# DMA transposes for q and x, smaller stores on GpSimd's queue, and row tiles of 128 in a fused attention and convolution kernel

**The chip, the cores and the metric.** One core of a Trainium2 chip. The metric is the device time of one execution in microseconds (us). With one core a run is called fast or slow by its own kernel only: slow is more than 1.5% above the fastest run of the same kernel. A ratio is the mean time of one kernel's fast runs over that of the other's of the same rounds, so it is not quite the ratio of the medians that are quoted. A run's first figure is the median of all its runs, slow ones too.

## The reference

Eight batches of linear attention (8 heads, 576 rows, 64 columns) feed a gated long convolution over the 576 rows. Cut to what matters:

```python
def phi(x, c, s):                       # c, s: cos and sin of pi/2 * row / 576
    r = np.maximum(x, 0.0)
    return np.concatenate([r * c, r * s], axis=-1)
kv  = einsum('bhsf,bhsd->bhfd', phi(k), v);  z = phi(k).sum(axis=2)
num = einsum('bhsf,bhfd->bhsd', phi(q), kv)
x   = (num / (phi(q) @ z + 1e-6)).transpose(0, 2, 1, 3).reshape(B, S, 512)
x1, x2, x3 = split(x @ w_proj, 3)
y   = x1 * irfft(rfft(x2) * rfft(filter)) * x3
out = y @ w_out                         # (8, 576, 512), float32
```

## The kernel before

Each batch goes through one pipeline: loads on GpSimd's queue (they cast to 16 bits), phi on VectorE, the transposes of q on TensorE, num, a "fold" of the attention result into frequency order (which also gives the x of the gate), x2, dft, the gate matmuls, the inverse, y, out, and stores. The parts that the change and the argument touch:

```python
def load_qk(b, nm, hs=slice(0, NH)):
    ...                                              # one load of 96 partitions
    nc.gpsimd.dma_start(out=raw_t[(b, nm)][:, hs],
        in_=src[b, hs].rearrange("h (p j) d -> p h (j d)", j=NJ))

def emit_qt(b, hp):                                  # q: transposed on TensorE, 12 of them
    for hh in range(2):
        for j in range(NJ):
            nc.tensor.transpose(u[:, hh, ds(j * NP, NP)], qp[:, j, 2 * hp + hh]..., perm)
    ...                                              # then two copies out of PSUM

def emit_out(b, grps=OG):
    ov = out[b].rearrange("(p j) n -> j p n", j=6)
    ...
        os_ = late["p"].tile([128, ng, DM], FP32, tag=f"os{ng}", bufs=2 * ng, ...)
    ...                                              # at most 96 rows, one leading dimension
            src = os_[x - OT[t] : e - OT[t], t - grp[0]]
            dst = ov[jb, p_a:p_b]
            q_ = nc.scalar if b >= B - 2 and t % 2 == 1 else nc.sync
            q_.dma_start(out=dst, in_=src)
```

Of the kernel before, what the change touches and what calls it, by code (L numbers as in the profile page):

```python
# [17 lines left out]
def kernel(  # L18
# [15 lines left out]

    nc = tc.nc
# [6 lines left out]
    NT = 5  # L42
# [25 lines left out]
    tcol = consts.tile([128, NJ], FP32, tag="tcol", name="tcol")  # L68
    epsc = consts.tile([128, NT], FP32, tag="epsc", name="epsc")
    perm = consts.tile([NP, NP], FP16, tag="perm", name="perm")  # L70
# [5 lines left out]
    fm = consts.tile([128, 24, 10], FP16, tag="fm", name="fm")  # L76
    tre = consts.tile([NP, 3, NP], FP16, tag="tre", name="tre")
    tim = consts.tile([NP, 3, NP], FP16, tag="tim", name="tim")

# [9 lines left out]
    qpt_buf = [consts.tile([128, NH, NT, 2, 64], FP16, tag=f"qpt{i}", name=f"qpt{i}") for i in range(1)]  # L89
# [24 lines left out]
    raw_t = {}  # L114

    def load_qk(b, nm, hs=slice(0, NH)):
        src = {"q": q, "k": k, "v": v}[nm]
        if hs.start == 0:
            rw = work.tile([NP, NH, NJ * D], FP16, tag="raw", bufs=4, name=f"{nm}raw{b}")
            raw_t[(b, nm)] = rw  # L120
        nc.gpsimd.dma_start(
            out=raw_t[(b, nm)][:, hs], in_=src[b, hs].rearrange("h (p j) d -> p h (j d)", j=NJ)
        )

    def emit_va(b, xs=range(4)):
        for x in xs:
            hs = slice(2 * x, 2 * x + 2)
            nc.scalar.copy(  # L128
                out=va_buf[b % 2][:, hs, :, 0:D],
                in_=raw_t[(b, "v")][:, hs].rearrange("p h (j d) -> p h j d", j=NJ),  # L130
            )
# [28 lines left out]
    def emit_iotas(part):  # L160
# [13 lines left out]
        iota("sr_i", [NP, QS], lambda t: [(t, [[2, 3], [12, NP // 2]], 1, 0)])  # L174

    def emit_cols():
# [6 lines left out]
        nc.vector.memset(warm, 0.0)  # L183
        sj = cc["s6_i"]
# [3 lines left out]
        nc.vector.tensor_tensor(out=tcol, in0=tcol, in1=scol, op=AL.mult)  # L188

        u16 = small("u16p")  # L190
        rnd(u16, p, 1.0 / 16.0, -15.0 / 32.0)
        dest = small("dest")
        tsc(dest, p, 6.0, AL.mult)
        nc.vector.scalar_tensor_tensor(
            out=dest, in0=u16, scalar=-95.0, in1=dest, op0=AL.mult, op1=AL.add
        )
        tsc(perm, cc["nrow_i"], dest[0:NP], AL.is_equal)

    def emit_pads():
        for va in va_buf:  # L200
            nc.vector.memset(va[:, :, :, D : D + 2], 1.0 / A1)
        for t in qpt_buf:
            nc.vector.memset(t[:, :, :, 0, 60:64], 0.0)
            nc.vector.memset(t[:, :, :, 1, 0:4], 0.0)

    def emit_fm():

        p = cc["p"]
        loc = small("loc")
        side = small("side")  # L210
        nc.vector.tensor_copy(out=loc[0:64], in_=p[0:64])
        tsc(loc[64:128], p[64:128], -1.0, AL.mult, 127.0, AL.add)
        nc.vector.memset(side[0:64], 1.0)
        nc.vector.memset(side[64:128], -1.0)
        lo = small("lo")
        rnd(lo, loc, 1.0 / 6.0, -5.0 / 12.0)
        li = small("li")
        nc.vector.scalar_tensor_tensor(
            out=li, in0=lo, scalar=-6.0, in1=loc, op0=AL.mult, op1=AL.add
# [3 lines left out]
        orb = small("orb", NT)  # L223
        for t in range(NT):
            tsc(orb[:, t : t + 1], lo, 10.0 * t, AL.add)
        oj = small("oj", NT)
        rnd(oj, orb, 1.0 / 16.0, -15.0 / 32.0)
        pos = small("pos", NT)

        tsc(pos, orb, 6.0, AL.mult)  # L230
        nc.vector.scalar_tensor_tensor(
            out=pos, in0=oj, scalar=-95.0, in1=pos, op0=AL.mult, op1=AL.add
        )
        nc.vector.scalar_tensor_tensor(
            out=pos, in0=li.to_broadcast([128, NT]), scalar=96.0, in1=pos, op0=AL.mult, op1=AL.add
        )
# [6 lines left out]
        orow_i = cc["orow_i"][:, 0:10]  # L243
        match = small("match", 10)
# [5 lines left out]
        for sl, (kk, c0) in enumerate([(0, 0.25), (3, 0.25), (1, 0.25), (1, 0.0), (2, 0.25), (2, 0.0)]):  # L250
# [4 lines left out]
        nc.scalar.activation(out=coef[:, 0:6], in_=ph, func=AF.Sin, scale=TWO_PI)  # L255
        tsc(coef[:, 3:6:2], coef[:, 3:6:2], 1.0 / R3, AL.mult)

        tsc(coef[:, 0:6], coef[:, 0:6], 2.0, AL.mult)
        tsc(coef[:, 0:6], coef[:, 0:6], RC, AL.add, -RC, AL.add)
        tsc(coef[:, 0:6], coef[:, 0:6], 0.5, AL.mult)  # L260
        tsc(coef[:, 6:12], coef[:, 0:6], side, AL.mult)
# [12 lines left out]
            in0=coef.unsqueeze(2).to_broadcast([128, 24, 10]),  # L274
            in1=match.unsqueeze(1).to_broadcast([128, 24, 10]),
# [23 lines left out]
    def emit_rows():  # L299
# [5 lines left out]
        par = cc["par"] = small("par")  # L305
        rnd(par, p, 0.5, -0.25)
        nc.vector.scalar_tensor_tensor(
            out=par, in0=par, scalar=-2.0, in1=p, op0=AL.mult, op1=AL.add
        )
# [10 lines left out]
    def emit_fwd_tables():  # L320
# [4 lines left out]
        u = small("u16")  # L325
        rnd(u, p, 1.0 / 16.0, -15.0 / 32.0)
        j = small("jr")
        nc.vector.scalar_tensor_tensor(
            out=j, in0=half, scalar=-3.0, in1=u, op0=AL.mult, op1=AL.add
        )  # L330
        w = small("w2s")

        tsc(w, p, 12.0, AL.mult, 1.0, AL.add)
        nc.vector.scalar_tensor_tensor(out=w, in0=u, scalar=-192.0, in1=w, op0=AL.mult, op1=AL.add)
        nc.vector.scalar_tensor_tensor(out=w, in0=j, scalar=2.0, in1=w, op0=AL.mult, op1=AL.add)
# [24 lines left out]
        for tb in (tre, tim):  # L360
            tsc(tb[:, 1:3], tb[:, 1:3], amp[0:NP], AL.mult)
            nc.vector.tensor_tensor(out=tb[:, 0], in0=tb[:, 0], in1=mask, op=AL.mult)

# [59 lines left out]
    def emit_h():  # L423
        hc, hs_, hb, alt = cc["hc"], cc["hs"], cc["hb"], cc["alt"]
        fa = filt16.rearrange("p x (j n) -> p x j n", j=3)
        for x, op in ((0, AL.add), (1, AL.subtract)):
            with behind("phi", 1, "k"):
                nc.vector.tensor_tensor(
                    out=feo[:, x].rearrange("p j n -> p (j n)"),
                    in0=filt16[:, 0], in1=filt16[:, 1], op=op,  # L430
                )
        for bl in range(3):
# [15 lines left out]
            tsc(h3[:, bl, 1], u[0:NP, 1], sc, AL.mult)  # L448
            nc.vector.tensor_copy(out=h3[:, bl, 2], in_=h3[:, bl, 1])
        u = unit("h_nyq")  # L450
        for j in range(3):
            nc.tensor.matmul(
                u[0:1, 0], alt[:, j % 2 : j % 2 + 1], feo[:, 0, j], start=(j == 0), stop=(j == 2)
            )
        nc.scalar.activation(out=h3[0:1, 0, 2], in_=u[0:1, 0], func=AF.Copy, scale=1.0 / S)
# [4 lines left out]
    def emit_phi(b, nm, h0=0, nh=NH):  # L460
        rw = raw_t[(b, nm)]
        dst = kp_t if nm == "k" else qp_t
        if h0 == 0:
            dst[b] = work.tile([NP, NJ, NH, 2, D], FP16, tag=f"{nm}p", bufs=2 if nm == "q" else 1, name=f"{nm}p{b}")
        t = dst[b]
        if nm == "q":

            tsc(
                t[:, :, h0 : h0 + nh, 0],
                rw[:, h0 : h0 + nh].rearrange("p h (j d) -> p j h d", j=NJ), 0.0, AL.max,  # L470
            )
        for j in range(NJ):
            for cs, col in ((0, ccol), (1, scol)) if nm == "k" else ((1, tcol),):
                mark["phi", b, nm] = tsc(
                    t[:, j, h0 : h0 + nh, cs], rw[:, h0 : h0 + nh, ds(j * D, D)],
                    col[0:NP, j : j + 1], AL.mult, 0.0, AL.max,
                )
# [20 lines left out]

    def emit_qt(b, hp):
        qp, qpt = qp_t[b], qpt_buf[0]  # L500
        u = psum.tile([128, 2, 1024], FP16, tag="u", bufs=4, name=f"qt{b}_{hp}")
        for hh in range(2):
            for j in range(NJ):
                nc.tensor.transpose(  # L504
                    u[:, hh, ds(j * NP, NP)],
                    qp[:, j, 2 * hp + hh].rearrange("p a b -> p (a b)"),
                    perm,
                )
        hsl = slice(2 * hp, 2 * hp + 2)
        ev = nc.scalar.copy if b == 0 and hp < 2 else nc.vector.tensor_copy  # L510
        mark["qpt", b, hp] = ev(  # L511
            out=qpt[:, hsl, :, 0, 0:60],
            in_=u[:, :, 0:300].rearrange("p h (t c) -> p h t c", c=60),
        )
        nc.scalar.copy(  # L515
            out=qpt[:, hsl, ::-1, 1, 4:64],
            in_=u[:, :, 276:576].rearrange("p h (t c) -> p h t c", c=60),
        )

    def emit_num(b, hp, wm=0):  # L520
        qpt, kvs = qpt_buf[0], kvs_t[b]
        if hp == 0:
            att_t[b] = work.tile([128, NT, DM], FP16, tag="att", bufs=2, name=f"att{b}")
# [3 lines left out]
        for hh in range(2):  # L527
            h = 2 * hp + hh
            for t in range(NT):
                nc.tensor.matmul(  # L530
                    u[:, hh, ds(t * 65, 65)], qpt[:, h, t].rearrange("p a b -> p (a b)"),
                    kvs[:, h // 4, ds((h % 4) * 65, 65)], start=True, stop=True,
                )
        nv = u[:, :, 0 : NT * 65].rearrange("p h (t e) -> p h t e", e=65)
        rcp = work.tile([128, 2, NT], FP32, tag="rcp", bufs=2, name=f"rcp{b}_{hp}")
        nc.vector.tensor_tensor(
            out=rcp, in0=nv[:, :, :, 64], in1=epsc.unsqueeze(1).to_broadcast([128, 2, NT]), op=AL.add
# [5 lines left out]
            in1=rcp.unsqueeze(3).to_broadcast([128, 2, NT, D]),  # L543
# [3 lines left out]
    def emit_fx(b, cs=range(NC), ccs=None, wm=0):  # L547
        att = att_t[b]
        if 0 in cs:
            fx_t[b] = work.tile([128, NC, 24, 48], FP16, tag="fx", bufs=2, name=f"fx{b}")  # L550
        fx = fx_t[b]
        for c in cs:
            u = unit(f"fx{b}_{c}")
            warm_up(u, wm)
# [325 lines left out]
```

## Time and profile before

| | before |
|---|---|
| time, median of 4 runs beside the changed kernel | 272.1 us (269.4 to 272.2) |
| start, first batch, four more batches, tail | 68.8, 30.3, 4 x 28.5, 58.1 us |
| TensorE, VectorE, ScalarE busy | 90%, 84%, 73% |

The batches are cut where the 48 small kv matmuls begin. The page's row of the DMA engines' busy share in 40 slices of the span, in tenths:

```profile
DMA  5999998919019296636860868114000600060235
```

### The profile page before, as it was taken

How to read it: one execution, taken by the hardware profiler on the slowest of the kernel's cores; microseconds unless marked ns; L12 is line 12 of the kernel's file. 1: busy time of each engine (PE TensorE's matmuls, PEld its weight loads, DVE VectorE, ACT ScalarE, POOL GpSimd, SP SyncE). 2: the span in 40 equal slices, each digit the busy share in tenths (PEclk: the TensorE clock that was granted, in tenths of full speed). 3: DMA queues.
4: the chain of work that ended last, by engine and by line, in shares of the span. 5: the costliest groups of instructions: out<-in, count | busy, mean ns of one | idle time of the engine just before them, and what ended most of it. 6: DMA issues, size and time to landing. Idle time of an engine off the chain costs nothing.

```text
span 271.2 us, 6320 instructions
## 1 busy us (share of the span) xinstructions
PE 243.0 (90%) x2457; PEld 175.2 (65%) x2457; DVE 226.9 (84%) x805; ACT 196.8 (73%) x274; POOL 27.3 (10%) x47
## 2 busy tenths in 40 slices
PE   0287998878989999999999999999999999999991
PEld 0164767547858776786678676867687768756830
DVE  7689997998899898979897989978997479646951
ACT  2279679798497778877897789786977667857630
POOL 8551111020020101110111011000000000000000
PEclk9999999995799999999999999999999999999998
DMA  5999998919019296636860868114000600060235
GB/s 79 168 206 205 206 205 122 166 14 169 3 14 161 33 230 90 89 40 152 150 101 3 174 128 124 16 51 125 0 2 9 169 2 0 2 174 13 69 117 155
DMA packets 26991, 26.70 MB, mean 98 GB/s; under 512 B 1680, under 2 KB 22160, under 8 KB 26960
## 3 DMA queue, kind: packets, MB, share of 16 engines
q0 software_dynamic: 21200, 16.84, 42.7%
q1 hardware_dynamic: 5120, 8.39, 10.7%
q10 hardware_dynamic: 640, 1.05, 1.3%
q8 instruction: 19, 0.31, 0.5%
q14 instruction: 12, 0.10, 0.1%
HBM read 33.69 MB, written 9.44 MB: 159 GB/s over the span
## 4 chain that ended last, share of the span: by engine, by line
PE 50%; ACT 22%; DVE 21%; DMA 4%; issue 1%; POOL 0%; SPq 0%; POOLq 0%; ACTq 0%
PE x L630 20%; PE x L593 9%; ACT x2f L598 7%; ACT va L128 7%; PE kv L491 5%; PE out L695 4%; PE fx L556 4%; DVE eo L672 4%; ACT fx L560 3%; DMA vraw<-in_v_dram 2%; DVE kp L99 2%; PE qt L504 2%; PE dft L607 2%; PE inv L657 2%; DVE qpt L511 2%; PE inv L656 2%
## 5 line engine op out<-in xcount | busy, mean ns | idle before, releaser
L630 PE MATMUL x<-fx,wp 128*128 128x288 f16 x512 | 67.5, 286 | 1.1 <-ACT fx L560 1.0
L630 PEld LDWEIGHTS <-wp 128*128 128x128 f16 x512 | 50.0, 98 | 13.3 <-issue 0.3
L593 PE MATMUL x<-wp,fx 128*96 128x512 f16 x192 | 45.2, 382 | 0.5 <-ACT x2f L598 0.5
L560 ACT CAST fx<-fx 128x960 f16<-128x960 f32 x32 | 30.6, 961 | 13.7 <-PE fx L556 13.7
L695 PE MATMUL out<-wo,y 128*128 128x512 f16 x160 | 37.6, 379 | 0.7 <-DVE y L677 0.7
L598 ACT ACTIVATE x2f<-x 96x1024 f16<-96x1024 f32 x24 | 24.5, 1020 | 14.6 <-PE x L593 14.6
L593 PEld LDWEIGHTS <-fx 128*96 128x96 f16 x192 | 22.4, 124 | 15.1 <-issue 0.8
L672 DVE TENSOR_TENSOR eo<-eq 128x144 f16<-128x144 f16 x128 | 23.7, 228 | 10.1 <-ACT eq L660 9.9
L128 ACT COPY va<-vraw 96x768 f16<-96x768 f16 x32 | 25.3, 827 | 9.3 <-DMA vraw<-in_v_dram 9.3
L638 DVE TENSOR_TENSOR g<-x,x1s 128x288 f16<-128x288 f32 x64 | 27.0, 448 | 1.3 <-PE x L630 1.1
L491 PE MATMUL kv<-va,kp 96*128 96x65 f16 x384 | 16.4, 202 | 11.7 <-ACT va L128 8.8
L540 DVE TENSOR_TENSOR att<-num,rcp 128x640 f16<-128x640 f32 x32 | 26.1, 820 | 0.3
L515 ACT COPY qpt<-qt 128x600 f16<-128x600 f16 x32 | 20.4, 671 | 7.5 <-DVE qpt L511 7.5
L695 PEld LDWEIGHTS <-y 128*128 128x128 f16 x160 | 14.9, 97 | 16.0 <-DVE y L677 1.2
L609 ACT CAST xf<-dft 96x1024 f16<-96x1024 f32 x24 | 23.5, 1010 | 2.2 <-PE dft L607 1.2
L491 PEld LDWEIGHTS <-kp 96*128 96x128 f16 x384 | 15.3, 104 | 13.3 <-DVE kp L99 8.1
L504 PEld LDWEIGHTS <-qp 96*128 96x128 f16 x384 | 20.2, 102 | 5.1 <-issue 1.1
L636 ACT CAST x1s<-x 128x576 f16<-128x576 f32 x32 | 20.5, 639 | 4.2 <-PE x L630 3.1
L612 DVE TENSOR_TENSOR m<-xf,h 96x1024 f16<-96x1024 f16 x24 | 16.3, 678 | 7.8 <-ACT xf L609 7.7
L504 PE MATMUL qt<-perm,qp 96*128 96x96 f16 x384 | 21.7, 213 | 0.5 <-ACT fx L560 0.3
L700 ACT ACTIVATE os<-out 128x1024 f32<-128x1024 f32 (+1 forms) x21 | 18.3, 883 | 5.2 <-PE out L695 5.1
L556 PE MATMUL fx<-fm,att 128*128 128x240 f16 x128 | 18.8, 270 | 2.2 <-DVE att L540 1.1
(185 smaller groups left out, 419.4 us busy)
## 6 DMA issues: line engine op xcount, KB each, us to landing
out_dram<-os SPq DMA_DIRECT2D x22, 192.0 KB, 2.5
qraw<-in_q_dram POOLq DMA_DIRECT2D x7, 576.0 KB, 6.6
kraw<-in_k_dram POOLq DMA_DIRECT2D x7, 576.0 KB, 6.3
vraw<-in_v_dram POOLq DMA_DIRECT2D x7, 576.0 KB, 6.5
out_dram<-os SPq DMA_DIRECT2D x20, 128.0 KB, 2.4
wp<-in_moe_w_proj_dram POOLq DMA_DIRECT2D x3, 512.0 KB, 12.3
out_dram<-os SPq DMA_DIRECT2D x22, 64.0 KB, 2.1
kraw<-in_k_dram POOLq DMA_DIRECT2D x2, 288.0 KB, 6.4
```

What stands on the lines that cost most here:

```text
L128: nc.scalar.copy(out=va_buf[b % 2][:, hs, :, 0:D], in_=raw_t[(b, "v")][:, hs].rearrange("p h (j d) -> p h j d", j=NJ),)
L491: nc.tensor.matmul(u[:, h // 4, ds((h % 4) * 65, 65)], kp[:, j, h].rearrange("p a b -> p (a b)"), va[:, h, j, 0:65], start=(j == 0), stop= ...
L504: nc.tensor.transpose(u[:, hh, ds(j * NP, NP)], qp[:, j, 2 * hp + hh].rearrange("p a b -> p (a b)"), perm,)
L540: mark["att", b, hp] = nc.vector.tensor_tensor(out=att[:, :, ds(hp * 128, 128)].rearrange("p t (h d) -> p h t d", h=2), in0=nv[:, :, :, 0: ...
L556: nc.tensor.matmul(u[:, t // 2, 0:480].rearrange("p (g o) -> p g o", o=20)[:, :, ds((t % 2) * 10, 10)], att[:, t, ds(c * 128, 128)], fm, s ...
L560: nc.scalar.copy(out=fx[:, c, :, 0:40].rearrange("p g (u o) -> p u g o", u=2), in_=u[:, :, 0:480].rearrange("p u (g o) -> p u g o", o=20),)
L593: nc.tensor.matmul(u[0:NP, comp], fx[:, c, ds(comp * 6 + 2 * bl, 2)].rearrange("p a b -> p (a b)"), wp16[:, c, ds(DM, DM)], start=(c == 0) ...
L598: mark["x2f", b, bl] = nc.scalar.mul(out=x2f[:, bl], in_=u[0:NP], mul=X2SC)
L630: nc.tensor.matmul(u[:, hf, 0:HS], wp16[:, i, ds(w * DM + c * 128, 128)], fx[:, i, ds(12 + 6 * hf, 6)].rearrange("p a b -> p (a b)"), star ...
L638: mark["g", b, c] = nc.vector.tensor_tensor(out=(g[:, c, 0:HS] if hf == 0 else g[:, c, HS:S][:, ::-1]).rearrange("p (j i o) -> p j i o", j ...
L672: nc.vector.tensor_tensor(out=eoh[:, a, :, ds(48 * x, 48)], in0=eqj[:, a, 0], in1=eqj[:, a, 1], op=op)
L695: nc.tensor.matmul(u[:, x], y[:, c, ds(OT[t], 128)], wo16[:, c], start=(c == 0), stop=(c == NC - 1),)
```

## The change

The intent is to take work off TensorE: q's 48 transposes and the fold's part for x go to DMA transposes, x2 uses full 128-row tiles, and narrow matmuls are put in pairs into different column groups. For this q is loaded with the even and the odd of its groups of six rows in separate partitions and transposed in 48-row pieces. The output rows of a row tile then belong to an even and an odd half, so the stores become smaller and more, and they move to GpSimd's queue. The core of a long diff (set-up tables, tile shapes and the order of emission are cut):

```diff
+    DMA_XT = 2
+    DMA_QT = 2
 def load_qk
+        if nm == "q" and b >= DMA_QT:
+            for e in range(2):
+                nc.gpsimd.dma_start(out=rw[ds(64 * e, 48), hs], in_=view[e::2])
 def emit_qt(b, hp)
+        if b >= DMA_QT:
+            e, half = hp % 2, hp // 2
+            nc.sync.dma_start_transpose(
+                out=qpt.rearrange("p h (j e m n) -> p (h j) e m n", ...)[:, :, e, half],
+                in_=qp[ds(64 * ((e + half) % 2), 48), half].rearrange("p h j a b -> p (h j a b)"))
+            return
+    def emit_xt(b):
+        nc.sync.dma_start_transpose(out=xt_t[b]..., in_=att_t[b]...)
 def emit_out
-        ov = out[b].rearrange("(p j) n -> j p n", j=6)
+        ov = out[b].rearrange("(k x y) n -> x y k n", x=2, y=6)
-                [128, ng, DM], FP32, tag=f"os{ng}", bufs=2 * ng, ...
+                ... FP32, tag="osl" if last else f"os{ng}", bufs=5 if last else ng, ...
-                    q_ = nc.scalar if b >= B - 2 and t % 2 == 1 else nc.sync
+                    q_ = nc.gpsimd if b < B - 2 else nc.sync
+                    if e - pos == 96:
+                        q_.dma_start(out=ov[:, m // 2], in_=sv[pos - OT[t] : e - OT[t]])
+                    elif t < 4 or last:
+                        q_.dma_start(out=ov[m % 2, m // 2, k0 : k0 + e - pos], in_=...)
+                    else:                            # 64 rows in two column halves
+                        for hf in range(2): q_.dma_start(...)
```

## The prediction

> **What bounds the kernel now.** I read the page first (busy shares), then the chain that ended last in order of time, then one table of windows cut at its repeating landmarks, then the groups by form inside one such window.
>
> ```profile
> PE 243.0 (90%) x2457; PEld 175.2 (65%) x2457; DVE 226.9 (84%) x805; ACT 196.8 (73%) x274; POOL 27.3 (10%) x47
> ```
>
> TensorE (PE) is busiest, but 90% of the span hides what happens in the middle. The chain shows a repeat: the 48 small kv matmuls come back every 28.5 us (127.58, 156.08, 184.58, 213.08). One repeat is one of the 8 batches.
>
> ```profile
> 94.41 0.51 PE qt L504 x12
> 94.92 1.73 PE out L695 x8
> ...
> 127.58 1.69 PE kv L491 x48
> 129.27 1.76 PE x L593 x8
> ...
> 137.45 1.96 PE x L630 x16
> 139.41 0.41 PE fx L556 x4
> ...
> 156.08 1.68 PE kv L491 x48
> ...
> 216.51 0.61 PE num L530 x20
> ...
> 259.38 1.03 ACT os L700
> 260.75 0.43 issue
> 261.61 2.06 DMA out_dram<-os
> 263.67 0.60 ACT os L702
> 264.30 0.70 DVE os L97
> 265.02 1.89 DMA out_dram<-os
> 266.91 0.69 DVE os L97
> ```
>
> A chain piece with a count gives the pitch, which is what a stream of overlapping matmuls really costs: 16 gate matmuls of 288 columns in 1.96 us are 0.1225 us each, though the groups give 286 ns as the mean of one. The windows, cut at the kv times, then give each engine's load in a batch (columns: us, PE, PEld, DVE, ACT, POOL busy with counts, clock, DMA share, GB/s):
>
> ```profile
> core 0: us, PE busy (x) PEld busy (x) DVE busy (x) ACT busy (x) POOL busy (x), PEclk, DMA share, GB/s
> 0.00:68.79 68.79, 51.02 (x531) 36.57 (x532) 61.00 (x265) 48.12 (x75) 18.51 (x36) 0.95 1.00 152
> 127.58:156.08 28.50, 27.89 (x302) 20.67 (x302) 25.68 (x85) 23.03 (x32) 2.32 (x3) 1.00 0.60 106
> 213.08:271.20 58.12, 51.13 (x420) 34.24 (x419) 35.44 (x112) 34.32 (x46) 0.00 (x0) 0.99 0.26 75
> ```
>
> So a batch is TensorE at 98%, VectorE (DVE) 90%, ScalarE (ACT) 81%, at full clock. The run is 68.8 us of start, five such batches (the first is 30.3), and a tail of 58.1, of which the last 11.8 (from 259.4) is storing: copies out of PSUM that wait for earlier stores to give back their buffers.
>
> **What the Trainium skill says.** (1) "TensorE: Matmul & The Clock Gate", Back-to-back issue gap, gives N/2.4 + 2.5 ns for a warm matmul of N columns: 122.5 ns at 288 and 215.8 at 512. The trace agrees (122.5; 1.73/8 = 216). (2) The same page, Part 3: Packing small matmuls, says that matmuls with few output rows run side by side when their outputs start in different column groups. No matmul of the kernel before does this. (3) "VectorE: DVE Perf Modes", Mode 2×_1P, says that packed 16-bit operands give two results a cycle, and that PSUM operands fall back to one. The trace agrees: for the same 288 elements the PSUM multiply takes 447 ns, the all-SBUF one 306.
>
> ```profile
> L638 DVE TENSOR_TENSOR g<-x,x1s 128x288 f16<-128x288 f32 x8 | 3.4, 447 | 0.0
> L675 DVE TENSOR_TENSOR y<-eo 128x288 f16<-128x288 f16 x4 | 1.2, 306 | 0.0
> L672 DVE TENSOR_TENSOR eo<-eq 128x144 f16<-128x144 f16 x16 | 3.0, 230 | 1.8 <-ACT eq L660 1.8
> ```
>
> (4) "DMA: Bandwidth & Descriptors", Latency and other measured facts, gives 261 GB/s for a DMA transpose; nothing in this trace shows one.
>
> **The change on TensorE, per batch from the third on.** Counts are from the instruction order of both kernels. *Gone:* the 48 transposes of q, 48 x 0.0425 (12 in 0.51) = 2.04 us; four DMA transposes replace them. *The fold (fx):* 16 matmuls of 240 columns (0.1025) and 4 of 192 (0.0825) = 1.97 become 24 of 96 columns; at the pitch of the 96-column transposes, 24 x 0.0425 = 1.02. It halves since x1 and x3 no longer come from it but from the attention result, which a DMA transposes. *x2:* 24 of 512 columns (5.2) become 16 full ones (3.5) and 4 of 64 rows in two column groups, 0.43 if they run in pairs and 0.87 if not. *dft:* 6 of 512 become 9, since row tiles of 128 do not match the 96-row frequency blocks: 1.3 to 1.95. *num:* 40 to 48, at 0.0305: 1.22 to 1.46. *out:* 20 of 512 (4.34) become 16 (3.47) and 8 of 64 rows by 256 columns, 0.44 paired or 0.87. *Unchanged:* gate 64 x 0.1225 = 7.84, kv 1.69, inv 32 x 0.0625 = 2.0. The sum goes from 27.6 (which explains the 28.5) to 23.8 paired, 24.7 unpaired. Nothing of this lies beside other TensorE work, so 2.9 to 3.8 us comes off the path as long as nothing else is slower.
>
> **VectorE, by pitch.** The q copies out of PSUM go: 4 x 0.39 = -1.6. g reads SBUF: 8 x (0.36 to 0.22) = -1.1. eo in 8 instructions of twice the size: 16 x 0.144 = 2.3 to 8 x 0.22 = 1.8, -0.5. att has 768 elements for 640 at about one a cycle: 4 x 0.13 = +0.5. Two of the va copies move here, +0.5. 25.7 becomes about 23.5.
>
> **ScalarE.** q copies 4 x 0.57 = -2.3; fx evictions (3.5 + 0.7) to 4 x 0.57, -1.9; two va copies -1.5; x2f -0.4; out -0.2; the x3s copies +2.2. 23.0 becomes about 19.
>
> **DMA.** A batch adds 4 transposes of 48 x 3072 and one of 96 x 3072 two-byte elements, 1.77 MB; at the skill's rate an estimate of 6.8 us of all engines. Today's share is 0.60 of 28.5 = 17.1, so 24 in all. Their latency should be hidden: q is prepared nearly a batch ahead (in the order its VectorE work stands in front of the preceding batch's attention), and xt is read a batch after its issue.
>
> **Ends.** The first two batches keep TensorE transposes and the fold for x1 and x3, so the start gains little: x2 -1 per batch, the g copies, against more setup (pads, masks, a second tangent column): -2. In the tail TensorE loses about 2.6 and the last tiles have five buffers and are halved over two engines, so the waits for stores (2.06 + 1.89) and the copies strung after them should go: -5.
>
> **Sum.** TensorE needs 23.8 to 24.7; VectorE with 23.5 is nearly as full, and two engines at 95% wait for each other more than one at 98% with 90% beside it. I take 25.5 per batch, 27 for the first: 67 + 27 + 4 x 25.5 + 50.5 = 246.5.
>
> **Rivals.** *A: DMA becomes the bound.* If transposes take twice the skill's rate, a batch has 31 us of DMA work and the kernel does not gain: 31 x 5 + 120 = 275. For it: 0.60 busy now, 256-byte pieces, and the first 68.79 us run at share 1.00 while moving only 152 GB/s. Against: loads wait for free buffers, not for engines, and a transpose between SBUF needs no HBM. *B: VectorE becomes the bound,* by q's relu with a reversed step or eo's 24-element runs falling out of the fast modes. Then a batch is 26.5 to 27 and the time 252 to 256. *C: the GpSimd queue stalls.* Loads and 14 small stores a batch share one in-order queue; a load behind a store that waits for ScalarE lands late and TensorE waits at kv or num. At 0.77 us an issue (the timeline's k and q loads) they fill 14 of 25 us; not a bound, but a late load could cost 1 to 3 us a batch: 250 to 260. *D: all pairs overlap and all waits hide:* 24 a batch and 240.
>
> **Range and chances.** Centre 246; D and a short tail give 237, B or C together with a slow start 259. A, or a transpose that is late every batch, is the way to no gain. Faster by over 2% (below 266.7) 0.88, within 2% 0.07, slower 0.05.
>
> **What would show it.** Right: kv of successive batches 24.5 to 26.5 apart; PE busy some 24 per batch and DVE 23 to 24; g near 300 ns; no wait of over 1 us for qpt or xt; pairs of 64-row matmuls starting within 10 ns. Wrong: PE waiting at num for the transposes or at the gate for xt; DMA share near 1 in the middle; DVE above 25 us a batch; POOL's stores delaying loads.

## The result, and the profile after

The changed kernel takes 308.8 us (307.5 to 309.6, 4 fast runs), the one before 272.1 in the same rounds: ratio 1.137, 95% interval 1.129 to 1.145. It is slower, far outside the range. Its page:

```profile
PE 227.1 (74%) x2333; PEld 154.4 (50%) x2333; DVE 213.9 (70%) x751; ACT 178.8 (58%) x275; POOL 80.4 (26%) x139
...
DMA  6999988999999599999999799994274480452231
...
q1 hardware_dynamic: 44202, 12.51, 34.3%
```

TensorE lost 16 us of work as meant, but is busy 74% instead of 90%. The DMA row now reads 9 nearly throughout to about 207 us (slice 27 of 40). The kv matmuls begin at 71.44, 94.94, 119.08, about 165.0, about 189.5 and 236.21, and the windows cut near there show two kinds of batch (same columns as in the prediction; a DMA share over 1 probably comes from records that overlap):

```profile
95.00:119.15 24.15, 24.15 (x272) 17.03 (x272) 19.82 (x59) 19.15 (x29) 11.15 (x19) 1.00 1.06 115
119.15:143.00 23.85, 3.79 (x62) 2.48 (x63) 7.60 (x28) 2.39 (x4) 7.64 (x14) 0.63 1.39 138
...
165.20:190.00 24.80, 24.80 (x292) 17.53 (x288) 19.23 (x58) 19.47 (x29) 11.72 (x19) 1.00 1.13 121
190.00:213.50 23.50, 2.88 (x39) 1.56 (x37) 7.58 (x28) 1.89 (x3) 7.10 (x13) 0.65 1.09 139
236.21:307.00 70.79, 51.63 (x438) 33.48 (x438) 35.34 (x101) 34.35 (x51) 15.40 (x28) 0.87 0.38 76
```

The first row is a batch as predicted: 24.15 us, TensorE busy all of it. The second and fourth are stalls of some 20 us with TensorE at 3 to 4 us; every second batch has one. What VectorE and ScalarE do of a batch falls partly into the stalls: over the five batches (71.44 to 236.21) they are busy 118.5 and 95.8 us, 23.7 and 19.2 a batch. The last row is the tail, 70.8 us for the 51.6 of TensorE in it, where before it was 58.1 for 51.1. What TensorE waits for, from the view of waits (us in total, times, longest):

```profile
PE num L594 <- DMA qpt<-qp: 40.7, 4, 15.7
...
PEld L594 <- DMA qpt<-qp: 26.6, 3, 15.9
```

And what SyncE did then, from its timeline (start, us from the first issue to the end of the last):

```profile
102.27 14.80 SPq L564 DMA_TRANSPOSE qpt<-qp  x3
117.16 13.04 SPq L643 DMA_TRANSPOSE xt<-att  x1
130.26 24.71 SPq L564 DMA_TRANSPOSE qpt<-qp  x4
```

The scheduler put three of a batch's four q transposes, then x's, then the fourth. Each issue is slow: x's holds SyncE for 13.04 us, where in experiment 4 below one took 3.1 us alone and 6.3 beside loads, each the mean of four. The fourth q transpose starts at 130.26, lands at 142.7, and num resumes at 142.78. By terms of the prediction's sum, in the profiled run:

| | predicted | after | difference |
|---|---|---|---|
| start | 67 | 71.4 | +4.4 |
| first batch | 27 | 23.5 | -3.5 |
| four batches | 102 | 141.3 | +39.3 |
| tail | 50.5 | 70.9 | +20.4 |

So the question is what makes the batches and the tail long. **Theories:** T, the work of the DMA transposes themselves; C, q's load, which stands behind 14 stores in GpSimd's in-order queue (it was issued 7, 14 and 10 us after q's buffer was free); later O, the order on SyncE's queue; and S, the form of the stores.

### The profile page after: what moved, and what is told of

The parts are those of the page before. It is cut to its first block, busy times and chain, and to the rows that moved or that the text cites. A ratio compares the mean times of both kernels' runs of the same rounds, so it can differ in the third digit from the quotient of the medians.

```text
span 307.1 us, 6174 instructions
## 1 busy us (share of the span) xinstructions
PE 227.1 (74%) x2333; PEld 154.4 (50%) x2333; DVE 213.9 (70%) x751; ACT 178.8 (58%) x275; POOL 80.4 (26%) x139
## 4 chain that ended last, share of the span: by engine, by line
PE 41%; DMA 25%; DVE 14%; ACT 7%; issue 4%; SPq 2%; POOL 2%; ACTq 1%; POOLq 0%; DVEq 0%
PE x L723 12%; PE x L658 8%; DMA out_dram<-os 8%; DMA qpt<-qp 7%; DMA qraw<-in_q_dram 7%; PE out L795 5%; PE num L594 3%; DVE kp L107 3%; PE kv L550 3%; PE dft L690 3%; SPq L643 2%; DMA vraw<-in_v_dram 2%; PE inv L759 2%; PE inv L760 2%; DVE att L604 2%
## 5 line engine op out<-in xcount | busy, mean ns | idle before, releaser
L723 PE MATMUL x<-xt,wp 128*128 128x288 f16 x512 | 68.6, 288 | 4.5 <-ACT os L839 3.8
L676 ACT ACTIVATE x2f<-x 128x1024 f16<-128x1024 f32 (+1 forms) x24 | 21.2, 882 | 62.5 <-PE x L658 62.5
L594 PE MATMUL num<-kvs,qpt 128*128 128x65 f16 (+1 forms) x384 | 18.6, 204 | 43.0 <-DMA qpt<-qp 40.7
L658 PE MATMUL x<-wp,fx 128*128 128x512 f16 (+1 forms) x160 | 40.1, 416 | 1.6 <-DVE qpt L580 1.0
L852 POOL DMA_DIRECT2D out_dram<-os x18 | 13.7, 762 | 72.0 <-ACT os L839 42.8
L604 DVE TENSOR_TENSOR att<-num,rcp 96x768 f16<-96x768 f32 x32 | 30.4, 949 | 0.4
L795 PE MATMUL out<-wo,y 128*128 128x512 f16 (+1 forms) x132 | 30.3, 379 | 0.0
L600 DVE TENSOR_TENSOR rcp<-num,epsc 96x12 f32<-96x12 f32 x32 | 5.2, 162 | 32.4 <-PE num L594 32.4
L854 POOL DMA_DIRECT2D out_dram<-os x42 | 22.6, 545 | 14.4 <-DMA vraw<-in_v_dram 10.1
L733 ACT CAST x3s<-x 128x576 f16<-128x576 f32 x32 | 20.4, 638 | 8.2 <-PE x L723 7.1
L748 DVE TENSOR_TENSOR g<-x3s,x1s 128x288 f16<-128x288 f16 x64 | 17.6, 299 | 10.3 <-ACT x3s L733 10.3
L636 ACT CAST fx<-fx 128x576 f16<-128x576 f32 x32 | 20.5, 640 | 5.1 <-PE fx L621 5.1
```

The costliest lines, as they stand in the source:

```text
L594: nc.tensor.matmul(u[0:m, hh, ds(t * 65, 65)], qpt[:, ds(h * S + t * NP, m)], kvs[:, h // 4, ds((h % 4) * 65, 65)], start=True, stop=True,)
L604: mark["att", b, hp] = nc.vector.tensor_tensor(out=att[:, :, ds(hp * 128, 128)].rearrange("p t (h d) -> p h t d", h=2), in0=nv[:, :, :, 0: ...
L636: mark["fx", b] = nc.scalar.copy(out=dst[:, c].rearrange("p g (j o) -> p j g o", j=3), in_=uf[:, 0:768].rearrange("p (j g o) -> p j g o", ...
L658: nc.tensor.matmul(dst, fx[:, c].rearrange("p g o -> p (g o)")[:, ds(128 * ch, n)], wp16[:, c, ds(DM, DM)], start=(c == cs[0]), stop=(c == ...
L676: mark["x2f", b, bl] = nc.scalar.mul(out=x2f[:, 2 * bl : 2 * bl + n], in_=u[:, 0:n], mul=X2SC)
L723: nc.tensor.matmul(u[:, hf, 0:HS], wp16[:, i, ds(w * DM + c * 128, 128)], xt[:, i, ds(6 * hf, 6)].rearrange("p a b -> p (a b)") if b < DMA ...
```

## The experiments

All are edits of the changed kernel; results are correct unless said otherwise.

**1. q on TensorE in all batches.**

```diff
-    DMA_QT = 2
+    DMA_QT = 8
```

> The changed kernel with q transposed on TensorE in all batches, xt still by DMA transpose. Theory T (the DMA transposes' own engine time is the bound: 44202 packets at 38 ns over 16 engines, 16.4 us a batch, two thirds of it q's, on top of 12 us of loads and 4 of stores): DMA work falls to about 22 us a batch, TensorE at 24.2 + 2.0 bounds again, about 253 us. Theory C (a chain of waits: q's load stands behind 14 stores in GpSimd's queue, so q, its transposes and num are late in every second batch): the load is as late as before, only the 10 to 13 us of transposing leave the chain, about 270 us. Neither expects more than 290.

304.6 us (ratio to before 1.113, 1.103 to 1.123). Both theories' figures are missed: without any q transpose by DMA little is gained, 7 us by the fast runs. The chain shows a new loop of about 31 us: a store, then q's load, then phi of q on VectorE, which stands ahead of y, then out, then stores.

**2. q and x both on TensorE.**

```diff
-    DMA_XT = 2
-    DMA_QT = 2
+    DMA_XT = 8
+    DMA_QT = 8
-            emit_xt(n)
+            if n >= DMA_XT:
+                emit_xt(n)
```

> The changed kernel without any DMA transpose: q on TensorE and x1, x3 from the fold, in all batches; row tiles, column tiles and stores on GpSimd's queue stay. T: DMA 16 us a batch, TensorE 24.2 + 2.0 + 1.0, ScalarE near 23.5: 256 to 262 us. C: q's load still behind the stores, so a stall of some us in every second batch stays: about 270 us.

290.5 us (1.075, 1.067 to 1.082). With no DMA transpose at all the kernel is still 20 us slower than before, and its tail still 70.4 us. T alone cannot be the cause.

**3. The stores on ScalarE's queue.**

```diff
-                    q_ = nc.gpsimd if b < B - 2 else nc.sync
+                    q_ = nc.scalar if b < B - 2 else nc.sync
```

> The changed kernel with the stores of the first six batches issued on ScalarE's queue in place of GpSimd's; all DMA transposes stay. T: the same bytes and packets, so nearly the same time, 298 to 312 us. C: q's load no longer waits behind the 14 stores (some 12 us of the chain in every second batch), so 275 to 285 us or less.

329.7 us (1.220). q's load is now early (VectorE waits 2.2 us for it in all), but ScalarE itself stops 41.1 us (kvs) until stores have landed. The stores' slowness moved with them, and on a busy engine it costs 21 us more.

**4. The DMA work alone** (wrong result, zeros).

```diff
+    for i in range(4): tr_x(i)      # then wait
+    for hp in range(4): tr_q(hp)    # then wait
+    for i in range(4): load(i)      # then wait
+    for i in range(4): load(i); tr_x(i)
```

> Wrong result on purpose (zeros): the DMA work alone. Four xt transposes of 96 x 3072 alone, then one batch's four q transposes alone, then four loads of 576 KB alone, then four xt transposes beside four such loads, then stores. T: an xt transpose lasts 5 us or more and a q transpose 2.7 or more with nothing else running, so a batch's transposes need 15 us or more; beside loads both together take about the sum of the two alone. C: transposes alone run near the 261 GB/s of the skill, 2.3 us an xt and 1.1 a q, and beside loads they hide: near the longer of the two.

The windows of the four parts:

```profile
2.49:17.00 14.51, 6.52 (x2) 0.00 (x0) 1.00 0.88 163
17.43:29.72 12.29, 0.03 (x1) 0.00 (x0) 1.00 0.63 96
30.20:45.03 14.83, 0.46 (x3) 3.16 (x4) 1.00 1.07 159
45.21:72.50 27.29, 0.38 (x5) 3.05 (x4) 1.00 1.13 173
```

A transpose of x takes 3.6 us alone (163 GB/s), a batch's four of q 12.3 (96 GB/s): 15.9 us of transposes a batch where the prediction estimated 6.8. Beside loads they add up (27.3 against 14.5 + 14.8), so nothing hides. For q's pieces this was not tried: alone they keep the engines busy at a share of 0.63 only, so beside other work they may cost less than 12.3. With three loads of about 2.9 us (the first of four took 6.2, the others 2.75 to 2.9) that makes 24.6 us a batch before any store, an estimate by adding the parts.

**5. q's load ahead of the stores.**

```diff
+    def store_held(b):              # the stores of an earlier batch, after the load of q
+        load_qk(b, "q")
+        for o_, i_ in held:
+            with behind("qload", b):
+                nc.gpsimd.dma_start(out=o_, in_=i_)
```

> All of the change is kept; q's load is put ahead of the 14 stores in GpSimd's queue for the batches 5 to 7, which is where it stood behind them (7, 14 and 10 us late). C (a q load that is late behind stores is the cause): the two stalls of about 20 us go, batches of 24.5 to 26 us, 265 to 275 us in all. O (a rival formed from the trace after: of the four q transposes of a batch the fourth was issued behind the transpose of x on SyncE's queue, whose issue took 13 and 16 us, and TensorE's num waited for the fourth, 15.7 us in the first stall) and T (DMA work of 28 us a batch against 24.15 on TensorE): nothing or little changes, 298 to 312 us, and TensorE's longest waits are still those for qpt.

308.7 us (303.0 to 312.1, one of four runs fast). q's load is now issued within 0.5 us of its buffer coming free, but in the profiled run the two batches with a stall still take 48.2 and 46.3 us. The median does not change, and the one fast run, 6 us below those of the changed kernel, is far from C's 265 to 275. As the cause of the stalls, C falls; a small gain is not excluded.

**6. The four q transposes together, then x's.**

```diff
-            emit_xt(n)              # after num of batch n
+            with behind("qdma", n + 1):
+                emit_xt(n)          # after the four transposes of the next q
```

> All of the change is kept; on SyncE's queue the four q transposes of the next batch stand ahead of the transpose of x, where after had three, then x, then the fourth. O: the fourth q transpose lands some 13 to 15 us earlier, the two stalls shrink by that, and the whole comes to about 278 to 288 us. T (DMA work of 28 us or more a batch, whatever the order): the wait only moves from q's transposes to x's (TensorE's gate matmuls or the fold then wait for xt), batches stay at 31 to 35 us on average, 298 to 312 us. C: no change, 305 to 312.

296.5 us (291.9 to 311.5; 1.086, 1.073 to 1.099). By the fast runs the order is worth some 15 us (308.7 to 294.1), less than O said, and part of the wait moved to x, as T said (the gate waited 7.0 us for xt).

**7 and 8. q on TensorE and all stores on SyncE; then staging tiles for two batches besides.**

```diff
-    DMA_QT = 2
+    DMA_QT = 8
-                    q_ = nc.gpsimd if b < B - 2 else nc.sync
+                    q_ = nc.sync
# the second run also: tag "os2" with bufs=4 (was 2), shared with the last batch
```

> q transposed on TensorE in all batches (304.6 us when this was the only edit), and besides all stores on SyncE's queue, which then carries only one transpose of x a batch. GpSimd's queue has loads alone. The loop seen in that run, stores then q load then DVE's qp then y then out then stores, about 31 us long, is cut. Chain theory: batches at TensorE's own work of about 25.7 us (24.15 plus 96 transposes of q), start 75, tail 65 to 70: 268 to 276 us. T: DMA work without q transposes is about 16 us a batch and binds nothing, so it expects the same here; with the 304.6 us run it tells only whether the store queue was the loop. If the batches stay at 31 us, the loop is not through GpSimd's queue.

> As the run before it (q on TensorE, stores on SyncE), and the output staging tiles for two batches rather than one (four tiles of two row tiles instead of two; the last batch takes them from the same set, so no memory is added). If the tail of 71 us (58 in the kernel before) was long because ACT waited for stores to free these tiles (5.5 us after a store of 7.5, twice in the chain), it comes 6 to 12 us below the run before it: 258 to 268 us. If the tail is long for another cause, within 3 us of it.

286.6 and 287.6 us (1.061 and 1.062). The loop is cut: batches are about 28.1 us, in which TensorE is busy 26.3 and VectorE 24 to 26 us. (A batch has 48 transposes of q, not the 96 of the expectation.) But the tail stays 70 us in both. In the second one TensorE's last matmul ends at 263.9, 3 us earlier than in the first, and the end stays at 285.3. So the tail is not a wait for staging tiles. Its chain and a window of it (columns as in the prediction) show what it is:

```profile
248.10 9.93 DMA out_dram<-os
...
258.71 8.43 DMA out_dram<-os
```

```profile
270.00:282.00 12.00, 0.00 (x0) 0.00 (x0) 0.00 (x0) 0.20 (x1) 0.00 (x0) 0.50 0.25 58
```

Single stores take 8 to 10 us from issue to landing, and with nothing else running they move 58 GB/s. By the packet records (the trace's list of the single pieces that DMA engines moved), exactly two packets are in flight for 8 of these 12 us; the share of 0.25 holds short stores that use more engines. The kernel before landed its stores of 192 KB in a median of 2.5 us (an expectation below says 2.2). The Trainium skill, "DMA: Bandwidth & Descriptors", Why a DMA increments its semaphore by 16 and not by 1, says how many of the 16 engines a DMA uses: the largest number up to 16 that divides the slowest dimension on both sides. A leading 2 makes that two engines, and with the some 27 GiB/s that the same page gives for one, an estimate of 58 GB/s. The trace agrees: mostly two packets at a time, and 58 GB/s with the short stores in it (51 in the steady part of experiment 13, where there are none). That the form is the cause is theory S.

**9 to 12. The stores of 2 x 48 rows split into two of 48.** First alone, then with the order of experiment 6, then on experiment 8, then with order and staging tiles.

```diff
-                        q_.dma_start(out=ov[:, m // 2], in_=sv[pos - OT[t] : e - OT[t]])
+                        for x_ in range(2):
+                            a_ = pos - OT[t] + 48 * x_
+                            q_.dma_start(out=ov[x_, m // 2], in_=sv[a_ : a_ + 48])
```

> All of the change is kept, but each store of 96 rows with a leading dimension of 2 (2 x 48 rows of 2 KB, 192 KB, three a batch) is issued as two stores of 48 rows. S, a theory formed from the last 20 us of the run with twice the staging tiles: TensorE is done at 263.9 of 285.3 us there, and the stores left move 50 to 58 GB/s, so a store with a leading 2 runs on two of the 16 DMA engines (the Trainium skill, DMA: Bandwidth & Descriptors, How many engines (k), says that k divides the slowest dimension) and takes 7 to 10 us, where one of 192 KB took 2.2 us in the kernel before. If S is the tail alone: tail 71 us to about 56, 292 to 298 us in all. If these stores also hold up the transposes and loads that need all 16 engines (S whole): batches of 24.5 to 26 and 250 to 262 us. T (28 us of DMA work a batch with no such store in it): 284 to 298. If the split does nothing, S is wrong: 305 to 312.

> As the run with the four q transposes ahead of x's (296.5 us), with the stores split as in the run before. S for the tail alone: 280 to 285 us. S whole: 247 to 258 us. T: batches at 28 to 31 us, tail 56: 272 to 285 us.

> As the run with q on TensorE, stores on SyncE and staging tiles for two batches (287.6 us), with the stores split. S: its batches of about 28.1 us stay (VectorE is busy 90% and more there), the 21 us between TensorE's last matmul and the end fall to 6 to 8, as in the kernel before: 272 to 275 us. If the split does nothing: 286 to 289 us.

> As the second run of these, with staging tiles for two batches. Stores that land in 2 to 4 us free the tiles in time, so it should be within 3 us of that run; if it is more than 5 us below, ACT's wait for the tiles mattered after all.

Means of the fast runs, with the median of all runs in brackets:

| run | without the split | with it | ratio to before |
|---|---|---|---|
| split alone | 308.7 (308.8) | 267.8 (273.0) | no interval, one run of four fast |
| split, order | 294.1 (296.5) | 262.9 (264.9) | 0.967 (0.958 to 0.976) |
| split, q on TensorE, SyncE, tiles | 287.6 (287.6) | 271.5 (271.4) | 0.998 (0.993 to 1.003) |
| split, order, tiles | not run | 262.8 (265.5) | 0.966 (0.959 to 0.974) |

Every kernel with the split is 16 to 41 us below the same kernel without it, though the bytes are the same and three more stores are issued a batch. The 41 rests on one fast run; the medians give 36. Where no q transpose competes (third row), all 16 us come from the tail: 70.5 to 54.3 us, batches unchanged. Where they do, the tail gains as much (70.9 to 54.3) and the batches the rest (five take 144.0 us instead of 164.8 in the two profiled runs, of which the one with the split is slow, 1.7% above that kernel's fastest). The staging tiles add nothing.

What is left against the predicted 246 shows in the fourth run's windows of its last three batches together and of the middle one; each of the three is 28.9 us long:

```profile
119.34:206.05 86.71, 77.83 (x810) 52.67 (x808) 75.03 (x239) 57.55 (x85) 30.96 (x59) 0.94 1.11 157
148.26:177.16 28.90, 26.00 (x272) 17.53 (x270) 20.57 (x64) 19.37 (x29) 10.73 (x21) 0.94 1.17 165
```

The DMA engines are full here, and 28.9 us is what experiment 4's 24.6 and the stores would make. That looks like T.

**13. The stores alone** (wrong result, zeros), one part after another.

```diff
+    three stores of 2 x 48 rows on SyncE;    then six of 48 rows on SyncE
+    three stores of 2 x 48 rows on GpSimd;   then six of 48 rows on GpSimd
+    (and each form on GpSimd beside a transpose of x)
```

> The stores measured alone (the output is zeros on purpose), each part waiting for the one before. S: one store of 2 x 48 rows (192 KB) on SyncE takes 8 to 9 us to land at 50 to 58 GB/s, the same rows in two stores of 48 rows 2 to 3 us; three stores of 2 x 48 rows take 11 to 14 us, six of 48 rows 3 to 5; on GpSimd's queue about the same, or 8 to 9 if its stores go to different engines. A transpose of x beside three stores of 2 x 48 rows lands after 9 to 14 us, if it needs the engines that they hold, beside six of 48 rows after 6 to 8, alone it took 3.6. Rival: the leading 2 costs nothing and 192 KB lands in 2 to 3 us in both forms; then what the split changed was something else, as the number of stores in flight.

Windows (us, VectorE, GpSimd, clock, DMA share, GB/s):

```profile
23.08:37.77 14.69, 0.00 (x0) 0.00 (x0) 1.00 0.11 40
38.18:42.57 4.39, 0.00 (x0) 0.00 (x0) 1.00 0.44 134
43.26:55.55 12.29, 0.00 (x0) 2.35 (x3) 1.00 0.24 49
56.23:61.05 4.82, 0.00 (x0) 3.02 (x6) 1.00 0.43 122
```

The same 576 KB take 14.7 us in one form and 4.4 in the other. The share of 0.11 is 1.8 of 16 engines, and by the packet records two packets are in flight for 11.7 of the 14.7 us, although three stores are waiting: S is shown for SyncE's queue. On GpSimd's the form costs nearly as much (12.3) with mostly two to six packets in flight; why that is no faster was not followed. A single store of 2 x 48 rows on SyncE moved its data until 6.4 us after its issue, less than the 8 to 9 expected. The part beside a transpose of x ended after 14.4 and 7.8 us, but in the first VectorE looked at the stores first, so the windows do not tell when that transpose landed. The packet records do: its 2,304 packets ran from 62.90 to 71.21 us beside the two-engine stores, from 77.78 to 82.33 beside the split ones, so 8.3 against 4.6 us beside the same bytes, where the first of experiment 4 took 3.0 alone. That two-engine stores hold up a transpose is thus seen once, on GpSimd's queue.

**14. x from the fold instead of by DMA,** on the fourth split run.

```diff
-    DMA_XT = 2
+    DMA_XT = 8                      # and no emit_xt
```

> The best version so far (stores split, the four q transposes ahead of x's, staging tiles for two batches; 265.5 us median, its last three batches 28.9 us each at a DMA share of 0.98) with x's transpose taken back to the fold on TensorE, so that a batch has some 3.6 us less of DMA work (four such transposes took 14.5 us alone) and TensorE about 1.5 us more. T (DMA work is what is left): those batches 25.5 to 27 us, 251 to 259 us. If the residue is the order or a wait of q's transposes rather than DMA work: within 3 us of 265.5.

259.2 us (0.951, 0.944 to 0.957; three of six runs fast, mean 257.2), within T's range by the fast runs. Four of the five batches are 24.6 to 25.2 us; one is 6.8 longer, in which num waited 4.5 for a q transpose that landed 17.2 us after its issue. The edit also takes x's transposes, which held SyncE for 5 to 9 us each, from in front of q's in SyncE's queue, so it does not separate DMA work from queueing.

**15. q on TensorE in batches 4 and 6 only,** on the same.

```diff
-    DMA_QT = 2
+    DMA_QT = (2, 3, 5, 7)           # with "in" for ">="
```

> The same version with q's transposes on TensorE in batches 4 and 6 only, so that DMA work falls by 12.3 us in every second batch and TensorE and VectorE gain some 1.6 and 2.5 us there. T: batches of 24.5 to 27 us, 250 to 258 us. If the residue is not DMA work: 262 or more.

265.4 us (0.976, 0.971 to 0.981): a miss for T. Three of its batches are 23.5 to 24.2 us, the other two 32.4 and 34.0, so less DMA work in every second batch did not help. That it comes in lumps would be one reading, not shown; the chain of the first long batch led over a load of k, the issue of the stores, q's load and y again.

**16 and 17. q's load ahead of the stores,** as in experiment 5, on 14 and on 15.

> The best version (259.2 us: stores split, four q transposes together, staging tiles for two batches, x from the fold), with q's load ahead of the stores on GpSimd's queue for batches 5 to 7. In that version one stall of 6.8 us was left, in which num waited for a q transpose that took 17.2 us. If q's load behind the stores still costs (C, which the same edit refuted while the slow stores were there): the stall shrinks, 252 to 257 us. If that stall is DMA work alone: no change, 256 to 262.

> The version with q on TensorE in batches 4 and 6 (265.4 us), with q's load ahead of the stores. There the two batches that follow such a q took 32.4 and 34.0 us, and the chain in them runs over stores, then q's load, then qp on VectorE, then y, then out: VectorE's qp for the next batch stands in front of y and waits for the load. C: those batches fall to 26 to 28 us, 252 to 258 us in all. If the load's place is not the cause: 262 to 268.

On 14: **253.3 us** (252.3 to 254.6, six fast runs; 0.935, 0.931 to 0.939), the best version, 6.5% below the kernel before. The long batch is gone. C, which made no clear difference while the two-engine stores were there, is worth 4 us without them by the fast runs (257.2 to 253.2; the medians differ by 6).

```profile
94.80:195.68 100.88, 100.88 (x1175) 72.36 (x1173) 93.73 (x297) 83.62 (x129) 42.76 (x79) 1.00 0.90 145
195.68:251.30 55.62, 50.15 (x464) 32.72 (x462) 35.41 (x102) 36.23 (x55) 16.81 (x34) 0.99 0.31 86
```

Four batches in 100.9 us with TensorE busy in all of it at full clock: TensorE is the bound again. On 15: 264.4 us (257.9 to 266.7, one of six runs fast), no gain that the spread would show (the one fast run is 6.6 us below the mean of the fast runs of 15). In the profiled run, a slow one, one of the two long batches fell from 32.4 to 28.2 us and the other rose from 34.0 to 39.2; there the gate waits 9.0 us for a transpose of x that took 22.4 and stood behind four of q. What else holds that version was not followed further.

## Why the prediction was wrong

**TensorE's sum was right.** 23.8 to 24.7 us a batch were predicted, 24.15 came in the batches that nothing else held up, and TensorE's mean over the five batches is 24.4. The pairs are part of it, and point (2) of the prediction holds: in 44 pairs of 64-row matmuls the two start 3 or 4 ns apart, and x2's four take 0.55 us for an expected 0.43 paired and 0.87 not. VectorE's 23.7 and ScalarE's 19.2 us a batch are the predicted 23.5 and 19, and in the best version VectorE is busy 93.7 of 100.9 us without being the bound: rival B did not come. The gate's multiply from SBUF takes 299 ns as expected. (What the prediction says of PSUM operands stands on its page under "The perf-mode tier table", not under the mode that it names.) Of rival D the pairs came, the hidden waits did not.

**The step of the ends failed:** "the waits for stores (2.06 + 1.89) and the copies strung after them should go: -5". The tail grew from 58.1 to 70.9 us, and with the stores split it was 54.2 to 55.6. TensorE's part of it fell as predicted (51.1 to 49.0), but the rest only from 7.0 to 5.3 us: even then some 2 of the 5 us came. The prediction counted the stores (14 a batch) and their issue time, but never the shape of their addresses. That was readable in the diff: the slowest dimension of the destination became 2. It is the largest single cause: the changed kernel is 36.7 us above the one before, and the split alone takes 36 off by the medians (41 by its one fast run). That it also lengthens batches came as a surprise, and by how much depends on what else is on the engines (16 us in all without q transposes, 31 to 41 with them).

**"An estimate of 6.8 us of all engines" failed.** The term was mis-sized: 15.9 us a batch (12.3 for q's 48-row pieces, 3.6 for x), from experiment 4. The prediction's own sum, 17.1 us from today's share plus this, would have been 33 us a batch instead of 24, more than TensorE's 24.15. Measured with the stores mended, the batches in which the DMA engines are full take 28.9.

**"Their latency should be hidden" failed** with it. "PE waiting at num for the transposes" was named as what would show the prediction wrong, and it is what TensorE did for 40.7 us. The order on SyncE's queue (three q transposes, x's, the fourth) made each wait longer; putting it right gave some 15 us with the slow stores and 5 without, the latter against a single fast run. "DMA share near 1 in the middle" and "POOL's stores delaying loads" came as well.

**Rival A** named 31 us of DMA work a batch and 275 us, "if transposes take twice the skill's rate". They take 2.3 times it, and the kernel with the stores mended but the order left takes 273.0 (267.8 in its fast run). That this is near 275 is partly luck: its five batches average 28.8 us and not 31, and start and tail take 127 and not 120. A should have had far more than a small part of the chances. **Rival C** was a real but small cost, 4 us, clear only when the larger ones were gone.

With stores split, q transposes and q's load in order, and x left to the fold, the sum reads 70.2 + 24.6 + 100.9 + 55.6 = 251.3 against the predicted 67 + 27 + 102 + 50.5: what was promised of the batches was there to be had. The start, 2 to 5 us over its term in every version with the DMA transposes of q, was not examined.

## What to carry to other kernels

When a layout change alters a store or a load, look at the slowest dimension of its address pattern before anything else; stores of the same bytes took 14.7 or 4.4 us by this alone. Work moved from a busy engine to DMA must be priced by measuring it alone and added to what the DMA engines already do, and the sum held against the new batch time. And a fix that shows nothing may be worth trying again after the largest cause is gone: q's load moved forward gave nothing clear first and 4 us later.

## What the Trainium skill lacked or had wrong

- "DMA: Bandwidth & Descriptors", Latency and other measured facts, gives 261 GB/s for a DMA transpose with a non-contiguous middle dimension. Here, SBUF to SBUF in 16 bits and alone, it was 163 GB/s for 96 x 3072 elements and 96 GB/s for pieces of 48 x 3072. The page has no dependence on the number of rows. (q's pieces also write shorter runs, 48 elements for 96, so the rows alone are not shown to be the cause.)
- The same page, Why a DMA increments its semaphore by 16 and not by 1, had the rule that mattered (a leading 2 gives two engines). No figure of its cost stands there: 14.7 us for three stores of 192 KB on SyncE's queue and 12.3 on GpSimd's, against 4.4 and 4.8 us for the same rows in six stores. Its list of rules speaks of fewer engines for a small outermost dimension, not of what one such store does to a busy kernel: here 16 to 41 us in some 300.
- No page was found to say how long a DMA transpose holds its issuing engine when the DMA engines are busy: one transpose's issue held SyncE for 3.2 to 4.1 us beside only stores, and for 13.0 us when the engines were full.
- "TensorE: Matmul & The Clock Gate", Back-to-back issue gap: the formula that the prediction takes from it is there the gap of an isolated matmul, and a stream of 512 columns is said to need about 131 ns each. In these traces a stream keeps to the formula: eight matmuls of 512 columns in 1.73 us, 216 ns each.
